# Unused stretches between the experts' operands: other distances modulo 512 bytes in a rounded float32 mixture of experts

## The chip, the cores and the metric

The kernel runs on one core of a Trainium2 chip. The metric is the device time of one execution in microseconds (us), as the median of several runs. The profile is one further execution of the same program, taken by the hardware profiler.

## What is computed

The reference filters a signal in the frequency domain and sends each token of the result through one of eight experts:

```python
X = np.fft.rfft(x, axis=1)                 # x: (8, 2496, 256)
Yr = Xr @ w_r - Xi @ w_i + b_r
Yi = Xr @ w_i + Xi @ w_r + b_i
Yr, Yi = soft_threshold(Yr, 0.01), soft_threshold(Yi, 0.01)
x = np.fft.irfft(Yr + 1j * Yi, n=2496, axis=1).reshape(19968, 256)
logits = x @ w_gate                        # 8 experts
expert_idx = np.argmax(logits, axis=1)
for e in range(8):
    xe = x[expert_idx == e]
    h = np.maximum(xe @ w1[e], 0.0)        # w1[e]: 256 x 1024
    out[expert_idx == e] = gate_w * (h @ w2[e])   # w2[e]: 1024 x 256
```

## The kernel before

The spectral part fills the first 450 us: transforms as matrix products, mixing with w_r and w_i (`mix`, L351), the inverse transform (`inv_a`, L418), routing, and a scatter of the rows by expert into DRAM. From then on, and alone after 596 us, the experts' tiles run. A tile is 512 tokens of one expert ("wide", 32 of them) or 256 ("narrow", 18 of them); three more narrow tiles at the end are run only if the routing needs them. The first three wide tiles (`early`) run while the last rows are still scattered.

Every float32 operand of the experts is split into a rounded part and a rest, both in the rounded float32 format that TensorE takes (`fp32r`): x into `xh2` and `xl2` (`upright`), w1 into `h1` and `l1` (`split1`), w2 into the two halves of `h2` (`split2`), and the hidden values into `hh` and `hl`, written by `up` itself.

- `up` (L882, its products at L904) makes the hidden values. For each of 8 blocks of 128 hidden units and each of 2 halves of the 256 inputs it issues three products: h1 with xh2, l1 with xh2, h1 with xl2. The weights are the stationary operand (128 columns, 512 bytes of each partition), the tokens the moving one (512 or 256 columns).
- `down` (L948, L962 to L965) makes the outputs. For each 128 tokens and each of 8 hidden blocks it issues one product of hh with both halves of h2 side by side (512 columns, L965) and one of hl with the first half alone (256 columns, L962 and, for the last block, L964). Here hh and hl are the stationary operands and h2 is the moving one. So there are 48 up products in each tile, and 16 down products for each 128 tokens: 64 in a wide tile, 32 in a narrow one.

TensorE's order is written out by hand (`manual_schedule`), as are those of ScalarE, VectorE and SyncE's queue in the stage of the experts: `step(t)` runs `up(t)` and `down(t)`, and while they run, ScalarE and VectorE split the operands of tile t+1.

The operands lie in two pools of SBUF. `home(t)` names the one of a tile's own operands: `w2p` for the early tiles and then every other tile, `hb` for the rest. hh and hl are always in w2p. A tile of a pool begins where the one before ended, in the order in which they are first asked for. In w2p that is three times xw (4224 bytes a partition), then h1, l1 (8192 each), xh2, xl2 (4096 each), hh, hl, h2 (16384 each); in hb it is xf, xh2, xl2, h2, h1, l1 behind the buffers of rows. All of these but xw are multiples of 512 bytes, and so are the steps from slice to slice within them. So all would begin at one remainder modulo 512. Three stretches are left unused: 160 bytes in hb ahead of the rows' xf ("space"), and in w2p 352 bytes ahead of hh ("space1") and 160 behind hl ("space2"). With them, every operand of both pools begins at remainder 416, and hh and hl begin at 256.

Of the kernel before, what the change touches and what calls it, by code (L numbers as in the profile page):

```python
# [10 lines left out]
F32 = mybir.dt.float32  # L11
F32R = mybir.dt.float32r
# [12 lines left out]
D = 256  # L25
E = 8
F = 1024
# [3 lines left out]
TT = 256  # L31
OOB = 1 << 20
RARE = 3
ROUND = 1.5 * 2.0 ** 23
EARLY = 3


def constants(nb):
# [60 lines left out]
class Kernel:  # L99
    def __init__(self, tc, nb, x, w_r, w_i, b_r, b_i, w_gate, w1, w2,  # L100
# [4 lines left out]
        self.cap = TT + self.ntok  # L105
        assert (nb - 2) * S - E * (2 * TT - 1) > (EARLY - 1) * 2 * TT
        self.early, self.psb = EARLY, None
        self.wide = -(-(self.ntok - E * (2 * TT - 1)) // (2 * TT))
# [653 lines left out]
    def open_experts(self, st):  # L762
        self.k2 = self.pool(st, "k2", 1, side="right")
        self.w2p = self.pool(st, "w2p", 1, side="right")
        self.psa = self.pool(st, "psa", 2, side="right", space=PSUM)
        self.hb = None
        self.r1 = [self.k2.tile([128, F], F32, name=f"r1{q}") for q in range(2)]
        self.r2 = [self.k2.tile([128, 4, D], F32, name=f"r2{q}") for q in range(2)]
        self.xqs, self.xrs, self.xts, self.ws, self.hs = {}, {}, {}, {}, {}
# [6 lines left out]

    def home(self, t):
        return self.w2p if t < self.early or (t - self.early) % 2 else self.hb

    def word(self, j, t, top):  # L780
        k = self.kind(t)
        t -= (0, self.early, self.wide)[k]
        return self.nc.sync.value_load(self.tabs[k][0:1, j, t:t + 1], min_val=0, max_val=top)
# [40 lines left out]
    def split1(self, t):  # L824
        if t >= self.nt:
            return
        nc = self.nc
        hi, lo = (self.home(t).tile([128, 2, F], F32R, tag=nm, name=nm) for nm in ("h1", "l1"))
        self.ws[t, 1] = (hi, lo)
        for q in range(4):  # L830
            c, s = q % 2, slice(q // 2 * 512, q // 2 * 512 + 512)
            v = self.r1[c][:, s]
            nc.scalar.copy(hi[:, c, s], v)  # L833
            nc.vector.tensor_sub(lo[:, c, s], v, hi[:, c, s])  # L834
            yield
        self.weights(t + 1, 1)

    def split2(self, t):
        if t >= self.nt:
            return  # L840
        nc = self.nc
        both = self.home(t).tile([128, 8, 2, D], F32R, tag="h2", name="h2")
        hi, lo = both[:, :, 0, :], both[:, :, 1, :]
        self.ws[t, 2] = both
        for q in range(4):
            s = slice(q * 2, (q + 1) * 2)
            v = self.r2[q // 2][:, q % 2 * 2:q % 2 * 2 + 2, :]
            nc.scalar.copy(hi[:, s, :], v)  # L848
            nc.vector.tensor_sub(lo[:, s, :], v, hi[:, s, :])  # L849
            yield  # L850
        self.weights(t + 1, 2)

    def upright(self, t):
        if t >= self.nt:
            return
        nc = self.nc
        n = self.length(t)
        if t < self.early:
            xf = []
            for c in range(2):  # L860
                p = self.psi.tile([128, 512], F32, tag="u", name="px", bufs=4)
                for h in range(4):
                    nc.tensor.transpose(p[:, h * 128:(h + 1) * 128], self.xrs[t][:, h, 8 + c * 128:136 + c * 128],
                                        self.ident)
                xf.append(p)
        else:
            xf = self.hb.tile([128, 2, 16, 32], F32, tag="xf", name="xf")[:, :, :n // 32, :]
            xq = self.xqs.pop(t)
            for lo in range(0, n // 32, 8):
                nc.vector.transpose(xf[:, :, lo:lo + 8, :].rearrange("p c t j -> p t c j"), xq[:, lo:lo + 8])  # L870
                yield
            xf = [xf[:, c].rearrange("p t j -> p (t j)") for c in range(2)]
        xh, xl = (self.home(t).tile([128, 2, 2 * TT], F32R, tag=nm, name=nm)[:, :, :n] for nm in ("xh2", "xl2"))
        for c in range(2):
            with self.tc.high_priority():
                nc.scalar.copy(xh[:, c], xf[c])
            with self.tc.high_priority():
                nc.vector.tensor_sub(xl[:, c], xf[c], xh[:, c])
            yield
        self.xts[t] = (xh, xl)  # L880

    def up(self, t, work=()):  # L882
        work = iter(work)
        nc = self.nc
        n = self.length(t)
        per = 2 * TT // n
        xh, xl = self.xts.pop(t)
        h1, l1 = self.ws.pop((t, 1))
        if t == 0:
            self.w2p.tile([128, 88], F32, name="space1")  # L890
        hh, hl = self.hs[t] = [self.w2p.tile([128, 8, 2 * TT], F32R, tag=nm, name=nm)[:, :, :n] for nm in ("hh", "hl")]
        if t == 0:
            self.w2p.tile([128, 40], F32, name="space2")
        for f2 in range(8 // per):
            if self.psb or f2 % 2 == 0:
                p = (self.psb if f2 % 2 else self.psa).tile([128, per, n], F32, tag="h", name="ph")
            else:
                p = self.psi.tile([128, 512], F32, tag="u", name="ph", bufs=4).rearrange("p (a n) -> p a n", a=per)
            for i in range(per):
                f = f2 * per + i  # L900
                m = 0
                for c in range(2):
                    for a, v in ((h1, xh), (l1, xh), (h1, xl)):
                        nc.tensor.matmul(p[:, i, :], a[:, c, f * 128:(f + 1) * 128], v[:, c, :],  # L904
                                         start=m == 0, stop=m == 5)
                        m += 1
            s = slice(f2 * per, f2 * per + per)
            with self.tc.high_priority():
                nc.scalar.activation(hh[:, s, :], p, AF.Relu)  # L909
                nc.vector.scalar_tensor_tensor(out=hl[:, s, :], in0=p, scalar=0.0, in1=hh[:, s, :],  # L910
                                               op0=ALU.max, op1=ALU.subtract)
            next(work, None)
            if t < self.early:
                self.tick(2)
                self.pace(hh.bitcast(F32)[0:1, f2, 0:1])
                self.send(2)
            else:
                self.tick(1)
        for _ in work:
            pass  # L920
# [127 lines left out]
```

## Time and profile before

| | us |
|---|---|
| median of 3 runs (1520.15 to 1521.5) | 1521.19 |
| the profiled execution, its own time | 1522.23 |
| its span, first to last instruction | 1520.4 |
| TensorE busy with products | 1496.1 |
| TensorE loading weights | 1313.4 |
| VectorE busy | 1105.4 |
| ScalarE busy | 943.0 |
| GpSimd busy | 439.6 |

A matmul instruction comes as two records: the load of the stationary operand (LDWEIGHTS, on the row "PEld") and the product (MATMUL, on "PE"). Products are pipelined: one begins while the results of the one before still drain, so that records overlap and their mean duration is longer than the distance between their starts. Where TensorE waits for nothing, the time of a stretch is read from starts: the start of the last less the start of the first, by the number of products between them. The granted clock is a share of TensorE's full 2.4 GHz. In the profile's names a trailing digit is left out, so that h1 and h2 read "h", l1 reads "l", and xh2 reads "xh".

### The profile page before, as it was taken

To read this page: it belongs to the slowest core of one execution; us is meant where nothing else is said; L and a number is where in the kernel's file an instruction comes from. 1 tells how busy PE (TensorE), PEld (TensorE's weight loads), DVE (VectorE), ACT (ScalarE), POOL (GpSimd) and SP (SyncE) were. 2 spreads that over 40 slices of the span, in tenths; PEclk is the share of its full clock that TensorE was granted. 3 is DMA by queue.
4 is the path that set the end of the run, shared out by engine and by line. 5 is a ranking of instruction groups with operands and counts; after the bars stand their busy time and mean duration, and the time that the engine had idled before them with its cause. 6 is when DMAs were issued, how large, how long until landed. Compare 5 with 4: busy or idle time off the path is not lost. (4 is left out here: it accounts for less than half of the span.)

```text
span 1520.4 us, 29861 instructions
## 1 busy us (share of the span) xinstructions
PE 1496.1 (98%) x9367; PEld 1313.4 (86%) x9367; DVE 1105.4 (73%) x2412; ACT 943.0 (62%) x2008; POOL 439.6 (29%) x527
## 2 busy tenths in 40 slices
PE   8999999999999999999999999999999999999997
PEld 4789899998989988888888888888888888998997
DVE  4678687777777987676766667666666666788885
ACT  2677777777777767455555555555555555676764
POOL 1101524435261635611221221122122112232232
PEclk9999999999999999999999999999999999999999
DMA  8953545546362314452232413322323243555421
GB/s 247 278 156 111 174 144 148 156 144 181 113 195 86 113 33 156 116 133 53 57 91 50 112 41 73 83 56 70 71 56 104 44 105 98 145 143 153 100 49 28
DMA packets 191518, 169.69 MB, mean 112 GB/s; under 512 B 117525, under 2 KB 159881, under 8 KB 191354
## 3 DMA queue, kind: packets, MB, share of 16 engines
q1 hardware_dynamic: 171390, 123.48, 31.9%
q0 software_dynamic: 19712, 43.75, 8.7%
q8 instruction: 76, 1.25, 0.4%
q14 instruction: 88, 0.72, 0.2%
q10 hardware_dynamic: 252, 0.50, 0.1%
HBM read 171.51 MB, written 66.37 MB: 156 GB/s over the span
## 5 line engine op out<-in xcount | busy, mean ns | idle before, releaser
L965 PE MATMUL po<-h,hh 128*128 128x512 f32 x1312 | 453.7, 393 | 0.0
L909 ACT ACTIVATE hh<-ph 128x512 fp32r<-128x512 f32 x328 | 196.1, 598 | 209.6 <-PE ph L904 189.2
L962 PE MATMUL po<-h,hl 128*128 128x256 f32 x1148 | 321.2, 280 | 0.0
L910 DVE SCALAR_TENSOR_TENSOR hl<-ph,hh 128x512 fp32r<-128x512 f32 x328 | 226.2, 691 | 125.8 <-ACT hh L909 117.9
L939 POOL DMA_INDIRECT out<-o,xr x116 | 139.3, 1201 | 501.1 <-DVE o L937 495.1
L904 PE MATMUL ph<-xh,l 128*128 128x512 f32 (+1 forms) x800 | 281.2, 351 | 1.0 <-DVE l L834 1.0
L904 PE MATMUL ph<-xh,h 128*128 128x512 f32 (+1 forms) x800 | 281.4, 352 | 0.3 <-ACT h L833 0.2
L904 PE MATMUL ph<-xl,h 128*128 128x512 f32 (+1 forms) x800 | 280.7, 351 | 0.0
L965 PEld LDWEIGHTS po<-h,hh 128*128 128x128 f32 x1312 | 238.4, 188 | 43.0 <-ACT hh L909 0.2
L962 PEld LDWEIGHTS po<-h,hl 128*128 128x128 f32 x1148 | 215.8, 188 | 6.0
L654 POOL DMA_INDIRECT xs_dram<-yb,pos x176 | 177.8, 1010 | 70.1 <-issue 35.3
L904 PEld LDWEIGHTS ph<-xh,l 128*128 128x128 f32 x800 | 151.3, 189 | 22.7 <-DVE l L834 1.6
L936 ACT ACTIVATE part<-po,xr 128x256 f32<-128x256 f32 x152 | 72.2, 475 | 156.5 <-PE po L965 156.5
L904 PEld LDWEIGHTS ph<-xl,h 128*128 128x128 f32 x800 | 151.3, 189 | 20.2
L904 PEld LDWEIGHTS ph<-xh,h 128*128 128x128 f32 x800 | 151.3, 189 | 19.9 <-ACT h L833 0.8
L937 DVE SCALAR_TENSOR_TENSOR o<-po,xr,part 128x256 f32<-128x256 f32 x152 | 73.3, 482 | 111.2 <-ACT part L936 108.9
L379 DVE SCALAR_TENSOR_TENSOR y<-v,r 64x256 f32<-64x256 f32 x320 | 133.8, 418 | 6.8 <-ACT r L373 1.6
L834 DVE TENSOR_TENSOR l<-r,h 128x512 fp32r<-128x512 f32 x200 | 128.1, 686 | 5.0 <-ACT h L833 3.5
L849 DVE TENSOR_TENSOR h<-r,h 128x512 fp32r<-128x512 f32 x200 | 127.8, 684 | 2.0 <-ACT h L848 1.3
L833 ACT CAST h<-r 128x512 fp32r<-128x512 f32 x200 | 112.2, 616 | 2.9 <-DMA r<-moe_w 2.8
L848 ACT CAST h<-r 128x512 fp32r<-128x512 f32 x200 | 112.3, 617 | 1.6 <-DMA r<-moe_w 1.6
L939 POOL DMA_INDIRECT out<-o,row x36 | 63.8, 1773 | 142.7 <-DVE o L937 136.6
(178 smaller groups left out, 2832.7 us busy)
## 6 DMA issues: line engine op xcount, KB each, us to landing
r<-moe_w SPq DMA_DIRECT2D x106, 512.0 KB
r<-moe_w SPq DMA_DIRECT2D x376, 128.0 KB
spec_dram<-ae SPq DMA_DIRECT2D x88, 240.0 KB
t<-spec_dram SPq DMA_DIRECT2D x160, 128.0 KB
x<-x SPq DMA_DIRECT2D x40, 384.0 KB
xq<-xs_dram SPq DMA_DIRECT2D x116, 128.0 KB
xq<-xs_dram SPq DMA_DIRECT2D x72, 64.0 KB
x<-x SPq DMA_DIRECT2D x35, 84.0 KB
```

The source lines that it names most:

```text
L379: nc.vector.scalar_tensor_tensor(out=y[q * 64:q * 64 + 64, kp, :], in0=u[h, q, :], scalar=LAM, in1=r[h, q, :], op0=ALU.add, op1=ALU.min)
L654: i = nc.gpsimd.indirect_dma_start(out=self.xs[:, :], out_offset=bass.IndirectOffsetOnAxis(ap=pos[:n, g:g + 1], axis=0), in_=y[:n, g, 0:XW ...
L833: nc.scalar.copy(hi[:, c, s], v)
L834: nc.vector.tensor_sub(lo[:, c, s], v, hi[:, c, s])
L848: nc.scalar.copy(hi[:, s, :], v)
L849: nc.vector.tensor_sub(lo[:, s, :], v, hi[:, s, :])
L904: nc.tensor.matmul(p[:, i, :], a[:, c, f * 128:(f + 1) * 128], v[:, c, :], start=m == 0, stop=m == 5)
L909: nc.scalar.activation(hh[:, s, :], p, AF.Relu)
L910: nc.vector.scalar_tensor_tensor(out=hl[:, s, :], in0=p, scalar=0.0, in1=hh[:, s, :], op0=ALU.max, op1=ALU.subtract)
L939: i = nc.gpsimd.indirect_dma_start(out=self.out[:, :], out_offset=bass.IndirectOffsetOnAxis(ap=at[h], axis=0), in_=o[:, h, :], in_offset=N ...
L962: nc.tensor.matmul(p[:, :D], hl[:, f - 1, hs], w2[:, f - 1, 0, :], start=False, stop=False)
L965: nc.tensor.matmul(p, hh[:, f, hs], w2[:, f].rearrange("p a d -> p (a d)"), start=f == 0, stop=f == 7)
```

## The change

Gap tiles of 32 to 448 bytes a partition, which nothing writes or reads, are put ahead of some operands, once for each pool and operand. A table gives the bytes. The two stretches "space1" and "space2" go away; "space" in hb stays.

```diff
+GAPS = {("w2p", "l1"): 32, ("w2p", "xh2"): 448, ("w2p", "xl2"): 64, ("w2p", "hl"): 320, ("w2p", "h2"): 160,
+        ("hb", "xl2"): 384, ("hb", "h2"): 160, ("hb", "h1"): 224, ("hb", "l1"): 32}
...
+    def place(self, pool, nm, shape):
+        n = self.gaps.pop((pool, nm), 0)
+        p = self.w2p if pool == "w2p" else self.hb
+        if n:
+            p.tile([128, n // 4], F32, name="gap_" + nm)
+        return p.tile(shape, F32R, tag=nm, name=nm)
+
+    def at(self, t, nm, shape):
+        return self.place("w2p" if self.home(t) is self.w2p else "hb", nm, shape)
...
-        hi, lo = (self.home(t).tile([128, 2, F], F32R, tag=nm, name=nm) for nm in ("h1", "l1"))
+        hi, lo = (self.at(t, nm, [128, 2, F]) for nm in ("h1", "l1"))
...
-        both = self.home(t).tile([128, 8, 2, D], F32R, tag="h2", name="h2")
+        both = self.at(t, "h2", [128, 8, 2, D])
...
-        xh, xl = (self.home(t).tile([128, 2, 2 * TT], F32R, tag=nm, name=nm)[:, :, :n] for nm in ("xh2", "xl2"))
+        xh, xl = (self.at(t, nm, [128, 2, 2 * TT])[:, :, :n] for nm in ("xh2", "xl2"))
...
-        if t == 0:
-            self.w2p.tile([128, 88], F32, name="space1")
-        hh, hl = self.hs[t] = [self.w2p.tile([128, 8, 2 * TT], F32R, tag=nm, name=nm)[:, :, :n] for nm in ("hh", "hl")]
-        if t == 0:
-            self.w2p.tile([128, 40], F32, name="space2")
+        hh, hl = self.hs[t] = [self.place("w2p", nm, [128, 8, 2 * TT])[:, :, :n] for nm in ("hh", "hl")]
```

The remainders of the operands' first bytes modulo 512, as the two built programs have them:

| pool | | h1 | l1 | xh2 | xl2 | hh | hl | h2 |
|---|---|---|---|---|---|---|---|---|
| w2p | before | 416 | 416 | 416 | 416 | 256 | 256 | 416 |
| w2p | after | 416 | 448 | 384 | 448 | 448 | 256 | 416 |
| hb | before | 416 | 416 | 416 | 416 | | | 416 |
| hb | after | 160 | 192 | 416 | 288 | | | 448 |

Instructions, their order and their waits are the same on every engine in both programs. A distance is written here as the remainder of the moving operand less that of the stationary one, modulo 512. In the spectral stage, which the change doesn't touch, the mixing products (L351) stand at 480, and the inverse products (L418) at several, since their operands zh and zl go round four buffers.

## Rows read from the trace of the kernel before

**Rows 1.** The page: busy time, share and instructions of each engine, and from its 40 slices the granted clock in tenths.

```profile
PE 1496.1 (98%) x9367; PEld 1313.4 (86%) x9367; DVE 1105.4 (73%) x2412; ACT 943.0 (62%) x2008; POOL 439.6 (29%) x527
...
PEclk9999999999999999999999999999999999999999
```

**Rows 2.** Windows of TensorE: the stretch and its length, busy time (records), granted clock, the DMA engines' busy share, GB/s. The first is in the bfloat16 warm-up, the second in the mixing products, the third in the wide tiles, the last spans the narrow tiles.

```profile
18.30:23.50 5.20, 5.20 (x25) 1.00 0.96 323
390.80:392.10 1.30, 1.30 (x13) 1.00 0.77 186
700.00:1300.00 600.00, 600.00 (x3059) 1.00 0.31 73
1305.50:1513.40 207.90, 205.46 (x1441) 1.00 0.41 106
```

**Rows 3.** Groups of TensorE's products in the tiles of the experts, by line and shape: count, busy time, mean ns of one, idle time before them.

```profile
L965 PE MATMUL po<-h,hh 128*128 128x512 f32 x1312 | 453.7, 393 | 0.0
L962 PE MATMUL po<-h,hl 128*128 128x256 f32 x1148 | 321.2, 280 | 0.0
L904 PE MATMUL ph<-xh,h 128*128 128x512 f32 x512 | 199.7, 390 | 0.0
L904 PE MATMUL ph<-xh,l 128*128 128x512 f32 x512 | 199.3, 389 | 0.0
L904 PE MATMUL ph<-xl,h 128*128 128x512 f32 x512 | 199.3, 389 | 0.0
L904 PE MATMUL ph<-xh,l 128*128 128x256 f32 x288 | 81.8, 284 | 1.0 <-DVE l L834 1.0
L904 PE MATMUL ph<-xh,h 128*128 128x256 f32 x288 | 81.7, 284 | 0.3 <-ACT h L833 0.2
L904 PE MATMUL ph<-xl,h 128*128 128x256 f32 x288 | 81.4, 283 | 0.0
L964 PE MATMUL po<-h,hl 128*128 128x256 f32 x164 | 45.7, 279 | 0.0
```

**Rows 4.** Timeline of TensorE over a wide tile: start in us, modelled duration, line, operation. The last down product of the tile before, the first two of 48 up products, the first three of 64 down products, the last of them, and the first up product of the next tile.

```profile
709.00 0.40 PE L965 MATMUL po<-h,hh 128*128 128x512 f32 x1
709.24 0.40 PE L904 MATMUL ph<-xh,h 128*128 128x512 f32 x1
709.47 0.39 PE L904 MATMUL ph<-xh,l 128*128 128x512 f32 x1
...
720.13 0.39 PE L965 MATMUL po<-h,hh 128*128 128x512 f32 x1
720.36 0.28 PE L962 MATMUL po<-h,hl 128*128 128x256 f32 x1
720.48 0.40 PE L965 MATMUL po<-h,hh 128*128 128x512 f32 x1
...
731.02 0.40 PE L965 MATMUL po<-h,hh 128*128 128x512 f32 x1
731.26 0.40 PE L904 MATMUL ph<-xh,h 128*128 128x512 f32 x1
```

**Rows 5.** The same over a narrow tile: its first up product, its first down product, the first up product of the next tile.

```profile
1316.87 0.28 PE L904 MATMUL ph<-xh,h 128*128 128x256 f32 x1
...
1322.62 0.39 PE L965 MATMUL po<-h,hh 128*128 128x512 f32 x1
...
1328.18 0.28 PE L904 MATMUL ph<-xh,h 128*128 128x256 f32 x1
```

**Rows 6.** Timeline of the weight loads at the start of the wide tile of rows 4: the loads for its second and third product.

```profile
709.24 0.19 PEld L904 LDWEIGHTS ph<-xh,l 128*128 128x128 f32 x1
709.47 0.19 PEld L904 LDWEIGHTS ph<-xl,h 128*128 128x128 f32 x1
```

**Rows 7.** Timeline of TensorE: a warm-up run of 24 bfloat16 products of 512 columns, each with its own weight load, as one merged row.

```profile
18.25 5.34 PE L546 MATMUL pw<-idle 128*128 128x512 bf16 x24
```

**Rows 8.** Timeline of TensorE: mixing products (sh and sl stationary, 256 columns moving), from the second of a run of twelve to the last.

```profile
390.85 0.28 PE L351 MATMUL pm<-wld,sh 128*128 128x256 f32 x1
390.96 0.28 PE L351 MATMUL pm<-whd,sl 128*128 128x256 f32 x1
...
392.03 0.28 PE L351 MATMUL pm<-whs,sl 128*128 128x256 f32 x1
```

**Rows 9.** Timeline of TensorE: inverse products (gh and gl stationary, 272 columns moving), from the second of two runs of three to the last.

```profile
326.10 0.28 PE L418 MATMUL py<-zh,gl 120*117 120x272 f32 x1
326.22 0.29 PE L418 MATMUL py<-zl,gh 120*117 120x272 f32 x1
...
326.60 0.29 PE L418 MATMUL py<-zl,gh 120*117 120x272 f32 x1
```

More of the change, by code (lines that the diff above doesn't have):

```diff
@@ L766, in open_experts @@
         self.hb = None
+        self.gaps = dict(GAPS)
         self.r1 = [self.k2.tile([128, F], F32, name=f"r1{q}") for q in range(2)]
```

## The prediction

> **What bounds the kernel now.** I read the engine shares first: TensorE is busy 98% of the span at a granted clock of nine tenths or more in every slice [rows 1]. Then the stretches: from 700 to 1300 us TensorE is busy for all 600.00 us, and in the narrow tiles for 205.46 of 207.90, at a granted clock of 1.00 [rows 2]. So in the expert stage nothing is waited for, and the time there is the number of products times the distance from one start to the next. Durations of matmuls in a table by line (389 ns for 512 columns [rows 3]) are no use for this, since one begins before the last has drained. I use starts.
>
> A wide tile runs 48 up products from 709.24 to 720.13, which is 226.9 ns each, and its 64 down products to 731.26, 11.13 us, which is 347.8 ns for a pair of 512 and 256 columns [rows 4]. At the full 2.4 GHz, 512 columns stream in 213.3 ns and 256 in 106.7. So an up product costs 13.5 ns more than its columns and a down product 13.9 on average. In a narrow tile the up products take 5.75 us for 48, 119.8 ns each or 13.1 over, and the down ones 5.56 us for 16 pairs [rows 5], 13.8 over each. Over 32 wide and 18 narrow tiles (1536 and 864 up products, 2624 down products [rows 3]) that is 32 x 1.54 + 18 x 1.07 = 68.5 us of start-to-start time beyond the columns. This is all that the change can act on.
>
> What are these 13 ns? The weights of the next product are loaded while the present one streams: the load for the product at 709.47 begins at 709.24 with the one before it [rows 4, 6]. So the two SBUF streams that run beside each other are the moving operand of one product and the stationary operand of the **next**. The bfloat16 warm-up does the same, and its 24 products of 512 columns take 5.34 us [rows 7] at clock 1.00 [rows 2], at most 222.5 ns each, and some 215 if the last drains as long as the up products do. So the rounded float32 products pay about 11 ns apiece that the bfloat16 ones don't, with the same loads.
>
> **The change, part by part.** Each engine issues the same instructions, with the same waits, in the same order; only addresses differ. Nothing is copied into the gaps and no transfer grows. Nine gap tiles replace two, which costs no time. ScalarE and VectorE write the same shapes to shifted addresses; I cost that at nothing, since TensorE waits for neither of them in these stretches [rows 2].
>
> Before, all tiles of the expert stage start at the same remainder modulo 512 except hh and hl. So the distance from a moving operand to the stationary operand loaded beside it is 0 in up, and 160 in down. After, in w2p, up has 448, 480 and 32 (beside l1, beside h1, then h1 of the next row block under xl2); in hb 224, 256 and 128. In down, hl under h2 stays at 160 in w2p and becomes 192 in hb; hh under h2 becomes 480 in w2p and 0 in hb.
>
> No row shows the experts at these distances. The nearest rows of the same kind of product are in the spectral stage. A run of twelve mixing products of 256 columns stands at 480 throughout: from 390.85 to 392.03 ten of them take 118 ns each, 11.3 over their columns [rows 8]. The inverse products of 272 columns have distances of 32 to 480 from one buffer to the next: 326.10 to 326.60, 125 ns each, 11.7 over 113.3 [rows 9]. Both lie 1.4 to 2.2 ns below what up pays at 0. I take 11.3, since the mixing run is, like up, long and unbroken.
>
> *Wide up products*: 1536 x (11.3 - 13.5) = -3.4 us. The upper bound is the only other distance at which a product of 512 columns is seen, 160 in down: 230 ns from 720.13 to 720.36 against 226.9 [rows 4], +4.8 us. The lower bound: the 11 ns beyond the bfloat16 pace gone altogether would be -17 us, but no rounded float32 run in the rows comes near it.
>
> *Narrow up products*: 864 x (11.3 - 13.1) = -1.6 us; bounds 0 and -1.6.
>
> *Down products*: the load of hl beside 512 columns is unchanged in w2p (160) and 192 in hb: nothing. The load of hh beside 256 columns now costs 120 ns [rows 4], of which the rest of the pair gives some back; at 480 I put it as unchanged or 0.5 ns worse for some 650, at 0 as up's 13.1 against an average near 11 in the down pattern (estimate: 27.8 a pair less the 16.7 of 230 ns), +2.0 ns for some 570: together +1.5 us. Bounds: the pair's 27.8 falling to twice 11.3 would be 1312 x -5.2 = -6.8 us; +3 ns on every pair, +3.9.
>
> *Tile switches*: the last down product, with the next tile's h1 loaded beside it at 0, takes 240 ns (709.00 to 709.24, 731.02 to 731.26) instead of 230 [rows 4]. After, the distance is 256 or 32. Some 45 x -9 ns = -0.4 us.
>
> The sum is -3.4 - 1.6 + 1.5 - 0.4 = -3.9 us. The profiled execution took 1522.23 us with a span of 1520.4; the sum goes on both. Against the median of the runs, 1521.19, it gives **1517.3 us**.
>
> The Trainium skill speaks against all of this. Its page "SBUF — State Buffer" (Who interferes with whom) gives TensorE two independent read ports, one for the moving operand and one for weight loads, and "TensorE: Matmul & The Clock Gate" (Step-by-step: what each phase is for) says that loading the next weights takes no read bandwidth from the running matmul. By that rule no distance matters. The second page also gives a start-to-start time of columns over 2.4 GHz plus about 2.5 ns (Back-to-back issue gap); the bfloat16 run agrees, the float32 products of the experts, 13 ns over, don't.
>
> **The rivals.** *No difference* (1521 us, within 3 us either way): the 13 ns belong to the rounded float32 product and not to addresses. For it: up at 0 and down at 160 pay nearly the same, 13.5 and 13.9 on average, although they stand at two distances [rows 4]; and wide up, narrow up and the down pairs all come out near 13.3, as if the excess were a fixed step. Against it: the mixing and the inverse products pay 11.3 and 11.7 [rows 8, 9] in the same mode. It also holds if terms cancel. The wide tile would then still take 22.02 us.
>
> *Slower* (1525.7 us): the 13.5 of wide up is already the best that 512 columns are given, because all operands are aligned alike and every product meets the same pattern; shifted, they fall to the pace that 512 columns have in down. That is 1536 x 3.1 = +4.8, narrow up -1.6, down +1.5, switches -0.4: +4.3 us, rounded up to +4.5 for starts read to 10 ns. It decides as soon as wide up averages above 228.5 ns. For it: 230 against 226.9 in one and the same tile. Against it: in down a product of 512 is always followed by one of 256 at 120 or less, and the pair averages what up does, so the 230 may be only the way in which the pair splits its time.
>
> *A large gain* (1510 us): all 5024 products fall by the 2.2 ns between up and the mixing run, -11 us. For it: nothing ties the mixing run's pace to its width. Against it: half of the down loads keep their distance or nearly so.
>
> *That gaps don't take effect* can't be: the built program has the shifted addresses.
>
> **How the numbers follow.** A measurement of this kernel tells about 0.2%, 3 us, from no change. The forecast, 3 to 7 us faster, has 0.31, the large gain 0.13, no difference 0.32, slower 0.24. So faster 0.44, same 0.32, slower 0.24. The forecast is the likeliest by its mechanism but not by much; no difference holds about as much, because my sum is only just beyond what can be told. The range runs from the large gain, 1510, to the slower case, 1525.7, taken to 1526; some 0.09 is left out on either side, for a gain nearer to the bfloat16 pace and for a pace worse than down's.
>
> **What would show it.** Right: the wide tile, start to start, at about 21.9 instead of 22.02 us in place of a fixed repeat, narrow up under 118.5 ns, down pairs within 3 ns of 347.8, and tiles of w2p and hb differing from each other by some ns, since their distances differ. Wrong by the second rival: wide up above 228.5 ns, narrow up gaining all the same. Wrong by the first: both homes at 226.9 and 119.8 as now. Any change in what TensorE waits for, or in the stage before 450 us, would say that something else than the distance acts.

## The result, and the profile after

The changed kernel takes 1533.06 us in the median of 4 runs (1532.70 to 1533.39), the kernel before 1521.35 (1520.15 to 1522.20, 4 runs). The ratio is 1.0073 with a 95% interval of 1.0057 to 1.0089: slower by some 11 us, where 4 us faster was forecast. It lies beyond the range, on the side of the second rival and further out than that rival put it.

TensorE waits for as little as before: the windows of its wide tiles and of its narrow ones (stretch, busy time and records, granted clock, DMA share, GB/s) read as in [rows 2].

```profile
700.00:1300.00 600.00, 600.00 (x3012) 1.00 0.30 71
1315.00:1524.30 209.30, 206.76 (x1455) 1.00 0.40 106
```

It is busy all of the time at the full clock and gets through fewer products in 600 us, 3012 records against 3059. So the starts have moved apart. The timeline of TensorE, from the first up product of a wide tile of w2p to the first of the next tile of w2p (the first four up products and the first down product of one, the first up and first down product of the tile of hb between):

```profile
869.90 0.39 PE L913 MATMUL ph<-xh,h 128*128 128x512 f32 x1
870.13 0.39 PE L913 MATMUL ph<-xh,l 128*128 128x512 f32 x1
870.36 0.40 PE L913 MATMUL ph<-xl,h 128*128 128x512 f32 x1
870.60 0.39 PE L913 MATMUL ph<-xh,h 128*128 128x512 f32 x1
...
880.99 0.40 PE L974 MATMUL po<-h,hh 128*128 128x512 f32 x1
...
892.24 0.40 PE L913 MATMUL ph<-xh,h 128*128 128x512 f32 x1
...
903.40 0.39 PE L974 MATMUL po<-h,hh 128*128 128x512 f32 x1
...
914.65 0.39 PE L913 MATMUL ph<-xh,h 128*128 128x512 f32 x1
```

These answer to [rows 4]. The 48 up products take 11.09 us in w2p and 11.16 in hb instead of 10.89: 231.0 and 232.5 ns each instead of 226.9. The down products take 11.25 in both pools instead of 11.13. The same rows of two narrow tiles answer to [rows 5]:

```profile
1362.39 0.28 PE L913 MATMUL ph<-xh,h 128*128 128x256 f32 x1
...
1368.02 0.40 PE L974 MATMUL po<-h,hh 128*128 128x512 f32 x1
...
1373.65 0.28 PE L913 MATMUL ph<-xh,h 128*128 128x256 f32 x1
...
1379.31 0.39 PE L974 MATMUL po<-h,hh 128*128 128x512 f32 x1
```

Here up did gain: 5.63 and 5.66 us instead of 5.75. Summed from the starts over all tiles (the last narrow down part, with no tile behind it, is left in the tail):

| stage, us | before | after | difference |
|---|---|---|---|
| ahead of the first up product | 595.9 | 596.8 | +0.9 |
| wide up, 32 tiles | 351.3 | 358.7 | +7.4 |
| wide down | 358.4 | 361.9 | +3.5 |
| narrow up, 18 tiles | 106.1 | 104.6 | -1.5 |
| narrow down, 17 of 18, and tail | 108.8 | 109.4 | +0.6 |
| span | 1520.4 | 1531.4 | +10.9 |

The first line is scatter: in the runs below it lies between 594.8 and 602.9, those on another chip, named below, left out. Products of the spectral stage run until then, and not only for the first 450 us. A down stage reaches to the first up product of the next tile, so the switch between two tiles is in it. The sums hold the waits too: by the spacing of the tiles without a wait, narrow up gained 2.0 us over its 18 tiles, and waits took 0.5 back.

### The profile page after: what moved, and what is told of

Same layout as the page of the kernel before. It is cut to its first block, busy times and chain, and to the rows that moved or that the text cites. A ratio compares the mean times of both kernels' runs of the same rounds, so it can differ in the third digit from the quotient of the medians.

```text
span 1531.4 us, 29859 instructions
## 1 busy us (share of the span) xinstructions
PE 1505.3 (98%) x9365; PEld 1312.1 (86%) x9367; DVE 1105.3 (72%) x2412; ACT 944.3 (62%) x2008; POOL 437.7 (29%) x527
## 3 DMA queue, kind: packets, MB, share of 16 engines
q1 hardware_dynamic: 171390, 123.48, 31.7%
```

## The experiments

"Excess" below is the mean distance from one start to the next, less the columns over 2.4 GHz, worked out from the starts of all products of a kind in a trace; starts after a wait and the last product of each up or down stage are left out. In all runs but those named otherwise the instructions, their order and their waits are those of the kernel before.

**Undoing one half at a time.** `undo_down` puts hh, hl and h2 back to 160, `undo_up` puts up back to 0:

```diff
 undo_down
+GAPS = {("w2p", "l1"): 32, ("w2p", "xh2"): 448, ("w2p", "xl2"): 64, ("w2p", "hh"): 320, ("w2p", "h2"): 160,
+        ("hb", "xl2"): 384, ("hb", "h2"): 128, ("hb", "h1"): 256, ("hb", "l1"): 32}
 undo_up
+GAPS = {("w2p", "hh"): 32, ("w2p", "hl"): 320, ("w2p", "h2"): 160, ("hb", "h2"): 32, ("hb", "h1"): 480}
```

> The changed kernel with the gaps around hh, hl and h2 set so that down stands at 160 again everywhere; up keeps its new distances. Summing starts in the two traces, the change cost wide up +7.3 us, narrow up -1.5, wide down +3.5, narrow down +0.5. Theory (the distance of the moving operand to the stationary one loaded beside it sets each product's time by itself): wide up stays near 11.09 us a tile in w2p and 11.17 in hb, down goes back to 11.14, the run takes 1533 - 4 = 1529 us. Rival (the shared alignment of the whole stage counts, and any break of it spoils up and down alike): down stays above 11.2 us although its own distances are those of before, and the run stays above 1531.

> The changed kernel with up back at distance 0 in both pools; down keeps its new distances (160 and 480 in w2p, 192 and 0 in hb). Theory (each product by its own distance): wide up back to 10.89 us, narrow up to 5.75, down stays at 11.25, the run takes 1533 - 7.3 + 1.5 = 1527 us, and with the other undoing the two parts add up to the whole. Rival (shared alignment): up stays slow in part, and the run lies above 1530.

Measured: `undo_down` 1528.27 us, ratio to before 1.0042 (1.0027 to 1.0057); `undo_up` 1526.17, 1.0024 (1.0013 to 1.0034). The timeline of a wide tile of w2p in each, first up product, first down product and the first up product of the next tile, in the second with the last down product ahead of it:

```profile
866.73 0.39 PE L912 MATMUL ph<-xh,h 128*128 128x512 f32 x1
...
877.83 0.39 PE L973 MATMUL po<-h,hh 128*128 128x512 f32 x1
...
888.96 0.39 PE L912 MATMUL ph<-xh,h 128*128 128x512 f32 x1
```

```profile
867.77 0.39 PE L912 MATMUL ph<-xh,h 128*128 128x512 f32 x1
...
878.67 0.39 PE L973 MATMUL po<-h,hh 128*128 128x512 f32 x1
...
889.69 0.39 PE L973 MATMUL po<-h,hh 128*128 128x512 f32 x1
889.91 0.39 PE L912 MATMUL ph<-xh,h 128*128 128x512 f32 x1
```

Up takes 11.10 us and down 11.13 in `undo_down`, 10.90 and 11.24 in `undo_up`. Summed from starts, wide up is 358.9 us in the first and 351.5 in the second, wide down 358.4 and 361.9. Each half keeps its own cost and gives the other's back, and the two ratios add up to 1.0066 of the 1.0073. The idea that a break anywhere spoils the whole stage falls.

**All distances kept, every address moved** (`shift_all`): up begins at 0 in w2p and at 256 in hb, hh and hl at 0, h2 at 160.

```diff
+GAPS = {("w2p", "h1"): 96, ("w2p", "h2"): 160, ("w2p", "o"): 256, ("hb", "xh2"): 352, ("hb", "h2"): 416, ("hb", "h1"): 96}
...
```

The three lines left out, which `scan1` to `scan4` have too, put a gap ahead of the output tile `o`.

> All distances of the kernel before (0 in up, 160 in down), but every operand of the experts begins elsewhere: up at remainder 0 in w2p and 256 in hb in place of 416, hh and hl at 0, h2 at 160. Theory (only the distance counts): 1521.4 us within 2, wide tiles of 22.03 us in both pools. Rival (the remainder of an operand's own address counts, and 416 is a good one): wide up above 228.5 ns a product in at least one pool and some 3 to 10 us more.

Measured: 1522.11 us, ratio 1.0001 (0.9991 to 1.0010). The timeline of a wide tile in each pool, first up and first down product:

```profile
868.61 0.40 PE L912 MATMUL ph<-xh,h 128*128 128x512 f32 x1
...
879.50 0.40 PE L976 MATMUL po<-h,hh 128*128 128x512 f32 x1
...
890.63 0.40 PE L912 MATMUL ph<-xh,h 128*128 128x512 f32 x1
...
901.52 0.40 PE L976 MATMUL po<-h,hh 128*128 128x512 f32 x1
```

10.89 us twice, as before. At these shifts an operand's own remainder doesn't count, only its distance to others.

**One distance for all kinds of up product**, another in each pool. Four kernels, in each h1 and l1 alike and xh2 and xl2 alike:

```diff
 scan1: up 256 in w2p, 160 in hb; down 0 and 320
+GAPS = {("w2p", "h1"): 256, ("w2p", "xh2"): 256, ("w2p", "hh"): 352, ("w2p", "o"): 160, ("hb", "h2"): 160, ("hb", "h1"): 192}
...
```

The tables of the others are left out here: `scan2` has up at 32 and 64, down at 32 and 96; `scan3` up at 96 and 128, down at 128 and 192; `scan4` up at 192 and 224, down at 224 and 256.

> Uniform distances that are not 0: all three kinds of up product at 256 in w2p and at 160 in hb, hh and hl alike at 0 in w2p's down and at 320 in hb's. Theory (0 is the good distance for 512 columns): wide up above 228.5 ns a product in both pools, as far as 230 to 233, narrow up at 116 to 119, and 1526 to 1535 us. Rival (what matters is that all kinds stand at one equal distance, whatever it is, so that products meet the same pattern each time): wide up at 226.7 ns again in both pools, and 1519 to 1523 us unless down is worse.

> Uniform distances again: up at 32 in w2p and 64 in hb, down at 32 in w2p and 96 in hb. Read from starts: 512 columns at 256 took 226.7 ns, as at 0, and at 160 234.0. Theory (the cost repeats every 256 bytes and only its multiples are cheap for 512 columns): wide up 229 to 236 ns in both pools, narrow up 115 to 119. Rival (any multiple of 64 is as good as 0, since lines of 64 bytes then begin together): wide up 226.7 in hb, and above 229 in w2p alone.

> Uniform distances: up at 96 in w2p and 128 in hb, down at 128 in w2p and 192 in hb. Theory (only multiples of 256 are cheap): wide up above 229 ns in both pools. Rival (multiples of 128): 226.7 in hb. For down, where 160 gives 347.8 ns a pair, the theory has no sign to give: between 346 and 354.

> Uniform distances: up at 192 in w2p and 224 in hb, down at 224 in w2p and 256 in hb. Theory (period of 256): wide up above 229 ns in both pools, and down at 256 as slow as it was at 0, some 31.7 ns over a pair's columns (351.7), while a period of 512 would let it come out at another figure than 0 did.

Measured: `scan1` 1529.92 us, ratio 1.0048 (1.0031 to 1.0065); the others, one run each beside 1521.07 for the kernel before, 1534.23, 1536.10 and 1535.04. The timeline of `scan1`, a wide tile of w2p (256) and one of hb (160), first up and first down product:

```profile
872.34 0.39 PE L912 MATMUL ph<-xh,h 128*128 128x512 f32 x1
...
883.22 0.40 PE L976 MATMUL po<-h,hh 128*128 128x512 f32 x1
...
894.46 0.39 PE L912 MATMUL ph<-xh,h 128*128 128x512 f32 x1
...
905.70 0.40 PE L976 MATMUL po<-h,hh 128*128 128x512 f32 x1
```

At 256 up takes 10.88 us, as at 0; at 160 it takes 11.24, 234 ns a product. Neither the theory nor its rival had that: one equal distance isn't enough (160 is one), and 0 isn't the only good one. The excess of up at every uniform distance, in ns:

| distance | 0 | 32 | 64 | 96 | 128 | 160 | 192 | 224 | 256 |
|---|---|---|---|---|---|---|---|---|---|
| 512 columns | 13.6 | 20.0 | 15.8 | 20.2 | 19.9 | 20.7 | 19.9 | 19.9 | 13.5 |
| 256 columns | 13.1 | 10.1 | 11.0 | 13.3 | 11.9 | 12.0 | 7.3 | 11.6 | 13.2 |

Products of 512 columns are cheap at multiples of 256 bytes and pay 2 to 7 ns more everywhere else, 64 being the mildest. Products of 256 columns have it nearly the other way round: 0 and 256 are among their dearest, and 192 costs only 7.3. The narrow tile of `scan4` in w2p, its first up product and its first down product, takes 5.45 us:

```profile
1363.69 0.28 PE L912 MATMUL ph<-xh,h 128*128 128x256 f32 x1
...
1369.14 0.39 PE L976 MATMUL po<-h,hh 128*128 128x512 f32 x1
```

For down, none of the uniform distances beats the 160 of before: a wide tile's down part takes 11.14 us there, 11.16 at 32 and 11.20 to 11.29 at the others (median of the tiles). At 256 a pair's excess is 30.7 ns and at 0 31.7, near to each other as a period of 256 would have it, but not equal.

**Half the weight load** (`half_load`): 64 stationary columns in each up product, 160 in w2p and 0 in hb. The kernel leaves out half of the hidden units; its table of gaps and the lines that make hh, hl and the down products follow are left out below.

```diff
-nc.tensor.matmul(p[:, i, :], a[:, c, f * 128:(f + 1) * 128], v[:, c, :],
+nc.tensor.matmul(p[:64, i, :], a[:, c, f * 128:f * 128 + 64], v[:, c, :],
...
```

> Up at 160 in w2p and 0 in hb, down at 160. Only 64 of 128 hidden units of each block are computed, so that each up product loads 64 stationary columns in place of 128 and streams the same 512; hh and hl hold 64 rows and down sums over them alone. Theory (the excess at a bad distance is the load and the stream in each other's way): wide up in w2p falls from 234 to 222 to 228 ns, since the load lasts half as long; in hb at 0 it stays or falls by less. Rival (the excess belongs to the moving stream and its product, not to the load beside it): 234 in w2p and 226.7 in hb as with full loads.

The whole took 1544.89 us, more than before, since each border between up and down now costs some 100 ns extra; the up products are read between such borders, from the first start to the last, 47 apart:

```profile
877.28 0.44 PE L912 MATMUL ph<-xh,h 128*64 128x512 f32 x1
...
887.98 0.39 PE L912 MATMUL ph<-xl,h 128*64 128x512 f32 x1
...
899.63 0.44 PE L912 MATMUL ph<-xh,h 128*64 128x512 f32 x1
...
910.49 0.39 PE L912 MATMUL ph<-xl,h 128*64 128x512 f32 x1
```

In w2p, at 160, 10.70 us or 227.7 ns a product, down from 234. In hb, at 0, it went up, to 231.1 ns, which the theory didn't allow. The first product of each stretch still has part of a border in it; without it the two are 227.0 and 230.1. The narrow products of hb fell to an excess of 6.9. The record of a load falls from 0.19 us [rows 6] to 0.13:

```profile
880.28 0.13 PEld L912 LDWEIGHTS ph<-xl,h 128*64 128x64 f32 x1
```

So the same moving streams with a shorter load beside them lose most of the penalty at 160. That the load takes part in it fits this, but isn't shown by this run alone, since its products also fill only half of the output's partitions. What is cheap at 0 isn't simply the absence of a conflict, since 0 got dearer with the shorter load.

**Shifts of a few bytes** (`fine`): xh2 and xl2 shifted inside longer tiles by 16 bytes in w2p and 8 in hb. As a row of such a tile has 2304 bytes in place of 2048, the products of the second half of the inputs stand at 272 and 264 instead, the same modulo 256.

```diff
+lo = 4 if self.home(t) is self.w2p else 2
+xh, xl = (self.home(t).tile([128, 2, 576], F32R, tag=nm, name=nm)[:, :, lo:lo + n] for nm in ("xh2", "xl2"))
```

> The kernel before, with xh2 and xl2 shifted inside longer tiles, by 16 bytes in w2p and 8 bytes in hb, so that up stands at distances of 16 and 8. Theory (a product of 512 columns is cheap only where both streams begin at the same place of a 256 byte period, to the byte or nearly): wide up 229 to 235 ns in w2p, and in hb somewhere between 226.7 and that. Rival (the period is cut into lines of 32 or 64 bytes and a shift within a line costs nothing): 226.7 ns in both pools.

The timeline, a wide tile of hb (8 bytes) and one of w2p (16):

```profile
875.64 0.40 PE L905 MATMUL ph<-xh,h 128*128 128x512 f32 x1
...
886.84 0.40 PE L966 MATMUL po<-h,hh 128*128 128x512 f32 x1
...
898.00 0.39 PE L905 MATMUL ph<-xh,h 128*128 128x512 f32 x1
...
909.11 0.40 PE L966 MATMUL po<-h,hh 128*128 128x512 f32 x1
```

11.20 us at 8 bytes, 233 ns a product, and 11.11 at 16, 231.5. Two words off are as bad as 160 bytes. The rival's lines of 32 or 64 bytes fall, unless the change between two distances in one tile (8 and 264) costs something by itself: 0 and 256 in turn were not run.

**Own weights or the next ones** (`own_or_next`): only l1 moved, so that for two of the three kinds the two distances differ.

```diff
+GAPS = {("w2p", "l1"): 352, ("w2p", "xh2"): 160, ("w2p", "hh"): 352, ("w2p", "h2"): 160, ("hb", "l1"): 480}
```

> The kernel before with l1 alone moved, so that xh2 less l1 is 160 in w2p and 32 in hb, and all else in up is 0. The first product of each three (h1 with xh2) then streams at 0 to its own weights and has l1 loaded beside it at 160 or 32; the second (l1 with xh2) streams at 160 or 32 to its own weights and has h1 loaded beside it at 0. Theory (the load that runs beside the stream counts, that is the next product's weights): from the first start to the second 231 to 236 ns, from the second to the third 226 to 229, wide up at 229 to 231 ns on average in both pools. Rival (a product's own weights count, at the time they are used): the first 226 to 229, the second 231 to 236.

The first four up products of a wide tile of w2p, and its first down product:

```profile
867.53 0.40 PE L912 MATMUL ph<-xh,h 128*128 128x512 f32 x1
867.76 0.39 PE L912 MATMUL ph<-xh,l 128*128 128x512 f32 x1
867.99 0.40 PE L912 MATMUL ph<-xl,h 128*128 128x512 f32 x1
868.22 0.40 PE L912 MATMUL ph<-xh,h 128*128 128x512 f32 x1
...
878.69 0.39 PE L973 MATMUL po<-h,hh 128*128 128x512 f32 x1
```

Up takes 11.16 us, 232.5 ns a product, nearly as much as with all at a bad distance; in one run the whole took 1527.89 us beside 1519.47. But neither side has its split. In w2p the excesses of the three kinds are 18.4, 19.3 and 20.1 ns, in hb 16.8, 20.7 and 17.4. The third kind, at 0 to its own weights and at 0 to the next, pays 20.1 in w2p. One operand out of four at a bad distance makes all three kinds pay.

What the next weights do is seen at the border alone, where the last up product of a tile has hh loaded beside it. In the same pool and the same repeating pattern of the wide tiles of w2p (means of 16 tiles), this product has an excess of 13.4 ns with hh at 0 (changed kernel) and 12.6 with hh at 192 (`undo_down`), and products of its kind have 21.6 with the next h1 at 32 everywhere else in the tile. In kernels with all of up at 0 it has 13.3 with hh at 0 (`shift_all`), 15.0 at 160 (before) and 21.7 at 480 (`undo_up`). From before to `undo_up` the product, its own weights and what ran ahead of it are the same, modulo 512; only the address of the next weights isn't. So the next weights count, but not they alone: with hh at 160 each time, the same place costs 15.0 ns in a tile with all of up at 0 or 256 and 24.1 in one at 160 (`scan1`).

One more rival can be read from these traces: that ScalarE and VectorE, which write the next tile's operands meanwhile, get in the way at the new addresses. In the tiles of hb, wide up products over which VectorE works all the time have an excess of 13.3 ns in the kernel before and 21.2 in `scan1`, those over which it is idle 14.3 and 19.2; for ScalarE it is 13.6 and 20.5, 13.3 and 21.0. The difference is there with either engine idle.

**Versions from what was found.** `narrow192` is the kernel before with the narrow tiles' up at 192 and the wide ones' at 0; `mix192` is the kernel before with a gap, ahead of the mixing constants, that moves the spectral mixing products from 480 to 192; `both192` has both. The kernel of the first takes columns 48 to 304 of its buffers:

```diff
 narrow192
+lo = 48 if n == TT else 0
+xh, xl = (self.home(t).tile([128, 2, 2 * TT], F32R, tag=nm, name=nm)[:, :, lo:lo + n] for nm in ("xh2", "xl2"))
 mix192
+f.tile([128, 56], F32, name="gap_w")
```

> The kernel before, with one edit: in narrow tiles xh2 and xl2 use columns 48 to 304 of their 512, so that the narrow tiles' up products stand at 192 while the wide ones stay at 0. Theory (the distance alone sets the time, and 256 columns at 192 ran at 113.7 ns each against 119.8 at 0): narrow up falls from 5.75 to 5.46 us a tile in both pools, 18 tiles give -5.2 us, and the run takes 1516 us, all else as before. Rival (the 113.7 of that one pool hung on its other operands or on w2p): less than half of it, and 1519 to 1522.

> The kernel before, with a gap of 224 bytes ahead of the mixing constants in the spectral stage, so that the mixing products stand at 192 in place of 480. Theory (192 is the good distance for runs of 256 columns anywhere): the twelve products after the bias go from some 118 to 114 ns, 1440 products give up to -6 us, some of it lost where that stage waits for other engines: 1515 to 1519. Rival (the spectral stage's pace is set by its waits, or the result belongs to the experts' operands): no change within 2 us.

> Both edits together. Theory: the gains add up, 1510 to 1515 us, below the kernel before by 0.4 to 0.75%. Rival: no more than the better of the two alone.

These three and `fine` ran on a chip on which the kernel before took 1556.39 us. In them the first up product comes 18 to 23 us later and the first two tiles are longer, the other wide tiles of the kernel before's length where their distances are its own; so only ratios to it are given: `narrow192` 0.9964 (0.9948 to 0.9981), `mix192` 0.9985 (0.9970 to 1.0001), `both192` 0.9969 (0.9953 to 0.9984). Two narrow tiles of `narrow192`, one in each pool, first up and first down product:

```profile
1357.44 0.28 PE L905 MATMUL ph<-xh,h 128*128 128x256 f32 x1
...
1362.92 0.39 PE L966 MATMUL po<-h,hh 128*128 128x512 f32 x1
...
1368.48 0.28 PE L905 MATMUL ph<-xh,h 128*128 128x256 f32 x1
...
1373.96 0.39 PE L966 MATMUL po<-h,hh 128*128 128x512 f32 x1
```

5.48 us in both pools instead of 5.75, as forecast: 18 x 0.27 = 4.9 us of the 5.6 measured. This version beats both kernels. In `mix192` the mean excess within the runs of mixing products, where they follow without a wait, fell from 12.0 to 9.8 ns, which is 2.4 us over some 1100 products. That is half of the fall that the theory had: 192 isn't worth as much to these products as to up. As a whole `mix192` is not clear of no change, and the two gains together measure no more than the first alone.

## Why the prediction was wrong

*Where the time is.* Right: TensorE waits for nothing in the tiles, the stage is products times their spacing, and the change acts on the spacing alone.

*Wide up products.* This is the step that failed. It put 11.3 ns, read on mixing products of 256 columns, in place of the 13.5 of 512 columns, for -3.4 us; the 512 columns went to 17.7 ns in w2p and 19.3 in hb, for +7.4 us. The width was not a detail. At the same distance 512 columns pay up to 13 ns more than 256 (19.9 against 7.3 at 192), and of the distances tried 0 and 256 are the only ones where the two pay alike. The kernel before stood at the best one for 512, and any other tried but 256 was a loss. The step's upper bound, 230 ns from the down products, was also too low: 231.0 and 232.5.

*Narrow up products.* Right, -1.6 forecast and -1.5 measured (-2.0 without waits). Here the width was that of the rows it was read from, but the distances weren't: one distance for all costs 256 columns between 7.3 and 13.3 ns, and that the three of each pool came to 10.5 and 11.2 ns, next to the 11.3, was in part luck.

*Down products.* The sign was right and the term mis-sized: +1.5 forecast, +4.1 measured with the tile switches in it, some +4.5 without. The step gave hl beside 512 columns nothing, at the 160 that stays in w2p and at 192 in hb. But the excess of these products rose from 16.7 to 19.8 and 21.0 ns. The 256 columns, to which the step gave the whole cost, hardly changed: 10.7 to 11.3 in w2p, with hh moved from 160 to 480, and 10.7 to 10.3 in hb, with hh at 0. So pricing each kind by the distance of the load beside it was wrong; in w2p the cost came up at a product whose own distance to that load stayed, as `own_or_next` has it for up.

*Tile switches.* The number is right: from 26 to 19 (hb) and 14 (w2p) ns of excess, some -0.4 us. The reason isn't: in `undo_up` the next h1 is back at 0 beside the last down product of w2p, and 23 of these 26 switches cost 13 or 14 ns, not 26. There that product's own hh still stands at 480 in place of 160, so the distance of the next weights didn't set the cost by itself.

*The rivals.* The second one had the mechanism, that wide up was already at the best place for 512 columns, and the sign; at 1525.7 it was too mild, 4.8 against 7.4 for up and 1.5 against 4.1 for down. The evidence that decided against it, that a pair in down averages what up does, was a coincidence of two distances, which no row separated: with both at 0 a pair has 31.7 ns (`scan1`, w2p), two up products 27. *No difference* falls: with the order and the waits unchanged, addresses alone cost 0.73%. The Trainium skill calls TensorE's two read ports independent ("SBUF — State Buffer", Who interferes with whom). The traces don't agree for these products: with hh alone moved, the product ahead of it went from 15.0 to 21.7 ns.

What stays open: why 512 columns need a multiple of 256 bytes and 256 columns don't, why a shorter load makes 0 worse, what a product's own weights cost beside the next ones, and how a pattern of several distances adds up. The runs show for up that 256 costs what 0 does; they don't show what in the memory has that period. Distances of hl and hh that differ from each other were tried in two pairs only.

## What to carry to other kernels

Read a cost per product only from products of the same width: here 512 and 256 columns want different places, and the best for one was among the worst for the other. In a stream of rounded float32 products, shift operands by a few bytes and read the spacing of starts over a long unwaited run; in this kernel 0.4% was gained by it and up to 1% lost. Before spreading operands apart, find out whether they already stand at the good distance, and keep every operand of the pattern there, since one that is off cost nearly as much as all.

## What the runs showed of the hardware that was not expected

- Up with rounded float32 operands costs 512 columns 13.5 ns at a distance of 0 or 256, 15.8 at 64 and 18 to 21 at the others, down to a shift of 8 bytes (20.1).
- 256 columns cost 7.3 ns at 192 and 13.1 to 13.3 at 0, 96 and 256.
- Several uniform patterns lie near multiples of some 6.7 ns: 13.5 and 19.9 to 20.7 ns for 512 columns, 6.9 to 7.3 and 13.1 to 13.3 for 256. Others don't (15.8, 10.1 to 12.0), and no run tests whether there is such a step. With half the load, 160 gives 512 columns 13.7, nearly the figure that full loads have at 0.
- The address of the weights loaded next counts: with hh at 0, 160 and 480 the last up product of a tile, all else in up at 0, has 13.3, 15.0 and 21.7 ns.
- The tiles repeat closely: with 0 and 160 a wide tile took 22.03 us in the trace of the kernel before and in that of `mix192`, although the kernel before took 2.3% longer as a whole on the chip of the second.
